# An attention block on one core: a shorter end, V evacuated by pairs, and the softmax offset in rows of its own

## The chip, the cores and the metric

The kernel runs on one core of one Trainium2 chip. The metric is the device time of one execution in microseconds (us). TensorE is called PE, VectorE DVE, ScalarE ACT, GpSimd POOL, and SyncE, whose queue issues most DMAs, SP.

## The reference

```python
B, S, D = x.shape            # 1, 2048, 448, bf16
H = 16; Dh = D // H          # 16 heads of 28
qkv = (x @ wqkv).reshape(B, S, 3, H, Dh).transpose(2, 0, 3, 1, 4)
q, k, v = qkv[0], qkv[1], qkv[2]
scores = jnp.einsum("bhqd,bhkd->bhqk", q, k) * (Dh ** -0.5)
p = softmax(scores, axis=-1)
o = jnp.einsum("bhqk,bhkd->bhqd", p, v)
return o.transpose(0, 2, 1, 3).reshape(B, S, D) @ wo
```

## The kernel before

The 16 heads form four groups `g` of four heads `i`. A head's 28 columns are padded to 32, so that a group fills 128 partitions. The 2048 queries form four blocks `c` of 512 and the keys 16 blocks of 128. A set is one group with one query block; there are 16 sets, and `ORDER` lists them with the last block of the group before the last moved to the second place from the end. Inside a set every head and key block is a unit, a 128 x 512 tile of scores; there are 1024 units.

Scores of a unit are products of `KA` (keys, scaled) with `QP` (queries): `emit_s`, L673. ACT takes two units at a time from a pair of PSUM banks and writes the exponentials `pt` (`do_exp`, L859). DVE takes units one by one from the banks `d0`, `d1` and sometimes `m`, and approximates the exponential by arithmetic on the bits: `do_a` (L874) writes `I`, and for every four units `do_add` (L897) writes two shifted copies `J`. Products with V (`do_pv`, L957) add an ACT unit with the weights `VA`, and a DVE unit three times, with `VA` and its scaled copies `VS`. The four heads of a group write to four column groups, 32 partitions each, of the bank `o`. `VA` holds a column of ones beside each head's 28 columns, so each head's row 28 of `o` is the softmax denominator.

The score has an offset taken off it: K carries four rows of ones (rows 28 to 31 of each head), and the Q side has one row, 28 + c, with a bound on the scores' size below a constant `OFFS`. That bound is computed by `qn_job` (L462): `bound` scales the norms by the largest key norm (`km2`, `z`), halves their bits for a root (`su`), adds `OFFS`, and `place` puts the row into `QP` by DMA (L486). `q_job` (L391) masks Q while it evacuates it (L410) and copies 28 rows of each head into `QP` by DMA (L416). `v_job` (L496) projects two key blocks into one bank, and `evac` copies them into `VA` with two instructions (L517 on DVE, L515 on ACT for three of the pairs).

A finished set is copied out of `o` (L986). A chain of small DMAs gathers its denominators, DVE inverts them, two more DMAs spread the reciprocals over the partitions, and POOL multiplies into `otile(g, c)` (L1008). Products with Wo of the first three query blocks are ordinary jobs (`oproj_job`, L542).

The order of the instructions is not written by hand. A planner in the kernel's own Python code keeps an assumed time for every engine and resource; each job is an `Op` with an assumed duration, needs, a priority and a bank. At each moment the engine that is free first picks what is ready. Whether a unit goes to ACT or DVE is decided in `dve_ok` by who would finish first. Each engine then runs its list in that order, with semaphores where one waits for another. When fewer products than wanted are ready, `dense` puts in a product with a zero operand (L703).

The last set is handled by hand behind the planner's loop (L1146 and on). Two DVE copies bring `o` to SBUF in halves (L1167). `early(tq)` multiplies the other three groups' outputs with Wo for one block of 128 queries (three products, L1163, twelve in all). The halves are transposed in fp32 (L1171), the denominators inverted (L1174) and multiplied (L1175), the result is transposed back in bf16 (L1181) and copied by ACT (L1182). Four products with Wo's last group (L1189) complete the four blocks, DVE and ACT copy them out (L1192, L1194), and two DMAs store them (L1195).

Of the kernel before, what the change touches and what calls it, by code (L numbers as in the profile page):

```python
# [7 lines left out]
ACT = mybir.ActivationFunctionType  # L8
# [29 lines left out]
def kernel(  # L38
# [58 lines left out]
    WO = big.tile([P, G, D], BF16, name="WO")  # L97
    VA = [[big.tile([P, GH, XB, P], BF16, name=f"VA{h}_{b}") for b in range(NXB)] for h in range(2)]
    VS = [[[big.tile([P, GH, XB, P], BF16, name=f"VS{k}_{h}_{b}") for b in range(NXB)] for h in range(2)]
          for k in range(1, NTERM)]  # L100
# [35 lines left out]
    for idx, funcs in enumerate(get_activation_tables(nc.m.arch, ()).values()):  # L136
        if ACT.Exp in funcs and ACT.Identity in funcs:
# [32 lines left out]
    nc.gpsimd.memset(qoff[:], 0.0)  # L170
    for i in range(HG):
        nc.gpsimd.affine_select(out=qoff[:], in_=qoff[:], compare_op=ALU.not_equal, fill=OFFS,
                                base=-(HP * i + Dh), pattern=[[0, 1]], channel_multiplier=1)
    for t in range(3):
        nc.gpsimd.memset(WRAW[t][:, :, D:D + WPAD], 0.0)

    def clear_v(h, b):
        nc.gpsimd.memset(VA[h][b][:], 0.0)
        nc.gpsimd.memset(VA[h][b][:].rearrange("p g t (i e) -> p (g t i) e", e=HP)[:, :, Dh:Dh + 1], 1.0)

# [8 lines left out]

    nc.gpsimd.tensor_copy(out=identf[:], in_=ident[:])  # L190


# [198 lines left out]
    def q_job(g, c, bank, pri, gate=0, split=2):  # L391
# [9 lines left out]
        def evac():  # L401
            if first:
                t = qtt[0] = wk.tile([P, QW], BF16, name="qt0", bufs=1)
            else:
                t = QAt[(g, c)] = big.tile([P, QW], BF16, name=f"QA{c}", tag=f"QA{c}", bufs=1)
            if first:
                nc.vector.tensor_scalar(out=t[:], in0=held[key][:, 0:QW], scalar1=qmask[:, 0:1],
                                        scalar2=qoff[:, 0:1], op0=ALU.mult, op1=ALU.add)
            else:
                nc.vector.tensor_scalar(out=t[:], in0=held[key][:, 0:QW], scalar1=qmask[:, 0:1], scalar2=None,  # L410
                                        op0=ALU.mult)

# [9 lines left out]
        add("DVE", 0.66, evac, need=[key + (split - 1,)], gives=[key], rel=(bank, 2) if first else bank,  # L422
            pri=pri)
# [38 lines left out]
    def qn_job(g, cs, bank, pri, gate=0):  # L462
# [8 lines left out]
        def bound():  # L471
            km2 = wk.tile([P, 1], F32, name="km2")
            nc.vector.tensor_scalar(out=km2[:], in0=kmt[g][:], scalar1=MARG ** 4, scalar2=None, op0=ALU.mult)
# [5 lines left out]
            nc.vector.tensor_scalar(out=su[:], in0=su[:], scalar1=OFFS, scalar2=None, op0=ALU.add)  # L479

# [11 lines left out]
        add("DVE", 1.6, bound, need=[key + (len(cs) - 1,)], gives=[("su",) + key], rel=bank, pri=pri, port=True)  # L492
        add("SP", 1.2 * len(cs), place, need=[("su",) + key] + [("QR", g, c) for c in cs],
            gives=[("QA", g, c) for c in cs], land=1.4, pri=1)

    def v_job(h, kt, bank, pri, gate=0, eng="DVE"):  # L496
# [12 lines left out]
        def evac():  # L509
            ps = held.pop(key)  # L510
            for part in range(2):
                src = ps[:, part * w:(part + 1) * w].rearrange("p (g i e) -> p g i e", g=GH, e=Dh)
                dst = VA[h][b][:].rearrange("p g t (i e) -> p g t i e", e=HP)[:, :, t0 + part, :, 0:Dh]
                if eng == "ACT":
                    nc.scalar.copy(out=dst, in_=src)  # L515
                else:
                    nc.vector.tensor_copy(out=dst, in_=src)  # L517
# [5 lines left out]
        add(eng, 0.62 if eng == "DVE" else 0.5, evac, need=[key + (1,)], gives=[key, ("V", h, kt + 1)], rel=bank, pri=pri)  # L523

    def vs_job(h, b, pri):
        def scale(k):
            nc.vector.tensor_scalar(out=VS[k - 1][h][b][:].rearrange("p g t e -> p (g t e)"),
                                    in0=VA[h][b][:].rearrange("p g t e -> p (g t e)"),
                                    scalar1=WT[k], scalar2=None, op0=ALU.mult)
# [410 lines left out]
    def do_pv(t, ws):  # L940
# [9 lines left out]
        for w in ws:  # L950
            for e in w:
# [4 lines left out]
                SETMM[key] = SETMM.get(key, 0) + 1  # L956
                nc.tensor.matmul(out=o[HP * i:HP * (i + 1), :], lhsT=vt[:, gg, j % XB, HP * i:HP * (i + 1)],  # L957
                                 rhs=e["ap"], start=(SETMM[key] == 1), stop=False, tile_position=(0, HP * i),
# [173 lines left out]

    while cur["oset"] < NSET or any(not late(op) for e in ops for op in ops[e]) or any(k[0] == "O" for k in held):
        e = min(free, key=lambda n: free[n])
# [14 lines left out]
    HW = QW // 2  # L1149
    a = pair_tile(s_bank())  # L1150
    b2 = pair_tile("a%d" % ((cur["u"] + 1) % 2))
    oT = [a[:, 0:QW], b2[:, 0:QW]]
    d0, d1, mb = bank_tile("d0"), bank_tile("d1"), bank_tile("m")
    banks = [d0[:], d1[:], a[:, QW:2 * QW], b2[:, QW:2 * QW]]
    spare = [[VS[k][0][hf][:].rearrange("p g t e -> p (g t e)") for hf in range(2)] for k in range(2)]
    osb_last = [spare[0][hf].bitcast(F32)[:, 0:HW] for hf in range(2)]
    rT = [wk.tile([P, 2, HG], F32, name=f"rT{hf}", bufs=1) for hf in range(2)]
    on = [wk.tile([P, HW], BF16, name=f"on{hf}", bufs=1) for hf in range(2)]
    OTf = [wk.tile([P, HW], BF16, name=f"OTf{hf}", bufs=1) for hf in range(2)]

    def early(tq):
        for gg in range(G - 1):
            nc.tensor.matmul(out=banks[tq][:, 0:D], lhsT=otile(gg, c)[:, tq * P:(tq + 1) * P], rhs=WO[:, gg, :],  # L1163
                             start=(gg == 0), stop=False)

    for hf in range(2):
        nc.vector.tensor_copy(out=osb_last[hf], in_=o[:, hf * HW:(hf + 1) * HW])  # L1167
    early(0)
    for hf in range(2):
        for k in range(2):  # L1170
            nc.tensor.matmul(out=oT[hf][:, k * P:(k + 1) * P], lhsT=osb_last[hf][:, k * P:(k + 1) * P], rhs=identf[:],  # L1171
                             start=True, stop=True)
        ov = oT[hf][:, 0:HW].rearrange("p (t h e) -> p t h e", h=HG, e=HP)
        nc.vector.reciprocal(out=rT[hf][:], in_=ov[:, :, :, Dh])  # L1174
        nc.vector.tensor_tensor(out=on[hf][:].rearrange("p (t h e) -> p t h e", h=HG, e=HP), in0=ov,  # L1175
                                in1=rT[hf][:].unsqueeze(3).to_broadcast([P, 2, HG, HP]), op=ALU.mult)
    early(1)
    tb = [mb[:].bitcast(BF16), bank_tile("o")[:].bitcast(BF16)]
    for hf in range(2):
        for k in range(2):  # L1180
            nc.tensor.transpose(out=tb[hf][:, k * P:(k + 1) * P], in_=on[hf][:, k * P:(k + 1) * P], identity=ident[:])  # L1181
        nc.scalar.copy(out=OTf[hf][:], in_=tb[hf][:, 0:HW])  # L1182
        early(2 + hf)
    rest = sorted({op.gives[0][2] for op in ops["PE"] if late(op)})
    for hf in range(2):
        osb = spare[1][hf][:, 0:2 * D].rearrange("p (t d) -> p t d", t=2)
        for k in range(2):
            tq = 2 * hf + k
            nc.tensor.matmul(out=banks[tq][:, 0:D], lhsT=OTf[hf][:, k * P:(k + 1) * P], rhs=WO[:, G - 1, :],  # L1189
                             start=False, stop=True)  # L1190
            if k == 0:
                nc.vector.tensor_copy(out=osb[:, k, :], in_=banks[tq][:, 0:D])  # L1192
# [44 lines left out]
```

## Time and profile before

| | |
|---|---|
| median of 3 runs | 371.97 us (371.8 to 371.98) |
| the profiled execution | 372.05 us, span 370.2 us |
| granted PE clock | 1.000 |
| busy: PE, DVE, ACT, POOL | 94%, 94%, 95%, 20% |
| instructions: PE, DVE, ACT, POOL | 3487, 648, 391, 93 |
| HBM | 7.58 MB read, 1.96 MB written |

The span goes from the first to the last instruction; the execution's own time is 1.85 us more. A row of a group shows line, engine, operation, what it writes and reads, shapes and count; then busy time in us and the mean of one in ns; then the engine's idle time just before, and what ended it. Busy time counts overlapping instructions of one engine once, so the mean of one can be more than busy time over count. Rows of a timeline and of the chain begin with start and length in us.

### The profile page before, as it was taken

What the parts mean: (1) busy time and instruction counts of PE and PEld (TensorE: products, weight loads), DVE (VectorE), ACT (ScalarE), POOL (GpSimd) and SP (SyncE); (2) the same over time, 40 slices, a digit from 0 to 9 for tenths busy, and PEclk for the clock granted to TensorE, in tenths of its full rate; (3) what the DMA queues carried; (4) which work ended last, traced back from release to release, by engine and by line L of the source; (5) the groups of instructions that cost most, each with busy time, mean ns of one, the idle gap of its engine ahead of it and who ended that gap; (6) DMA issues with size and microseconds to landing.
All of it is one profiled execution on the core that took longest, in us unless ns stands there. A gap on an engine that the chain in (4) does not pass through costs nothing.

```text
span 370.2 us, 8863 instructions
## 1 busy us (share of the span) xinstructions
PE 348.0 (94%) x3487; PEld 112.2 (30%) x3487; DVE 347.5 (94%) x648; ACT 353.0 (95%) x391; POOL 74.4 (20%) x93
## 2 busy tenths in 40 slices
PE   8899998999999999999899999989898999999995
PEld 5443322222333333232222222222222222222222
DVE  7899999999999899999999899999999999999993
ACT  4599999999999999999999999999999999999992
POOL 8931032243010512121010324201010101001010
PEclk9999999999999999999999999999999999999999
DMA  8410011011000001010000001100000001010101
GB/s 256 119 39 12 3 24 35 3 33 36 19 29 32 2 4 38 18 28 30 17 16 3 30 3 54 28 20 14 19 13 4 28 28 56 25 50 21 55 16 50
DMA packets 14994, 12.15 MB, mean 33 GB/s; under 512 B 6780, under 2 KB 13032, under 8 KB 14952
## 3 DMA queue, kind: packets, MB, share of 16 engines
q1 hardware_dynamic: 13400, 10.16, 9.4%
q10 hardware_dynamic: 1040, 1.02, 0.8%
q8 instruction: 27, 0.44, 0.5%
q0 software_dynamic: 512, 0.40, 0.5%
q14 instruction: 15, 0.12, 0.1%
HBM read 7.58 MB, written 1.96 MB: 26 GB/s over the span
## 4 chain that ended last, share of the span: by engine, by line
PE 43%; ACT 38%; DVE 10%; issue 7%; DMA 1%; DVEq 0%; SPq 0%; ACTq 0%
ACT pt L859 38%; PE a L673 16%; PE o L957 12%; PE m L260 5%; DVE I L874 3%; PE m L506 2%; DVE J L897 2%; PE o L590 1%; PE m L542 1%; PE o L703 1%; DVE KA L288 1%; DMA QP<-su 1%; PE d L673 1%; PE m L304 1%; PE a L260 1%
## 5 line engine op out<-in xcount | busy, mean ns | idle before, releaser
L859 ACT ACTIVATE pt<-a 128x1024 bf16<-128x1024 f32 x370 | 340.9, 1137 | 1.3 <-PE a L673 0.7
L874 DVE TENSOR_SCALAR I<-d 128x512 int16<-128x512 f32 x254 | 166.8, 681 | 7.3 <-PE d L673 6.2
L673 PE MATMUL a<-QP,KA 32*128 32x512 bf16 (+1 forms) x730 | 142.5, 381 | 13.3 <-ACT pt L859 12.1
L957 PE MATMUL o<-pt,VA 128*32 128x512 bf16 x740 | 108.3, 386 | 0.5 <-ACT pt L859 0.5
L897 DVE TENSOR_SCALAR J<-I 128x2048 int16<-128x2048 int16 x142 | 100.7, 741 | 0.1
L673 PEld LDWEIGHTS <-KA 32*128 32x128 bf16 (+1 forms) x1024 | 49.2, 91 | 148.5 <-issue 147.8
L673 PE MATMUL d<-QP,KA 32*128 32x512 bf16 x250 | 81.5, 384 | 0.0
L957 PE MATMUL o<-J,VS 128*32 128x512 bf16 x568 | 74.3, 384 | 1.7 <-DVE J L897 1.7
L957 PE MATMUL o<-I,VA 128*32 128x512 bf16 x284 | 66.9, 385 | 0.0
L1008 POOL TENSOR_TENSOR xs<-o_sb,rr 128x512 bf16<-128x512 f32 x12 | 16.6, 1381 | 107.7 <-DMA rr<-scr 92.5
L957 PEld LDWEIGHTS <-VA 128*32 128x32 bf16 x1024 | 24.3, 94 | 40.8 <-issue 40.6
L260 PE MATMUL m<-XT,WRAW 112*32 112x512 bf16 x384 | 29.6, 385 | 0.3 <-DVE QA L410 0.3
L270 POOL TENSOR_TENSOR sq<-QA 128x512 bf16<-128x512 bf16 x15 | 17.5, 1164 | 57.9 <-DVE QA L410 57.9
L270 POOL TENSOR_TENSOR sq<-KA 128x512 bf16<-128x512 bf16 x12 | 16.1, 1340 | 53.6 <-DVE KA L288 53.6
L874 DVE TENSOR_SCALAR I<-m 128x512 int16<-128x512 f32 x30 | 20.5, 682 | 0.9 <-PE m L673 0.6
L957 PEld LDWEIGHTS <-VS 128*32 128x32 bf16 x568 | 16.2, 94 | 15.7 <-issue 15.7
L506 PE MATMUL m<-WRAW,XT 112*128 112x224 bf16 x128 | 17.1, 261 | 0.2
L1008 POOL TENSOR_TENSOR OTL<-o_sb,rr 128x512 bf16<-128x512 f32 x3 | 3.8, 1271 | 60.0 <-DMA rr<-scr 60.0
L703 PE MATMUL o<-zero 128*128 128x512 bf16 x42 | 14.6, 387 | 0.0
L506 PEld LDWEIGHTS <-XT 112*128 112x128 bf16 x128 | 10.2, 97 | 7.1 <-issue 6.2
L673 PE MATMUL m<-QP,KA 32*128 32x512 bf16 x30 | 11.5, 384 | 0.0
L410 DVE TENSOR_SCALAR QA<-m,qmask 128x512 bf16<-128x512 f32 x15 | 11.2, 744 | 0.2 <-PE m L260 0.2
(113 smaller groups left out, 197.3 us busy)
## 6 DMA issues: line engine op xcount, KB each, us to landing
rr<-scr SPq DMA_DIRECT2D x15, 256.0 KB
QP<-QA SPq DMA_DIRECT2D x60, 28.0 KB
out_dram<-osb SPq DMA_DIRECT2D x12, 112.0 KB
WRAW<-in_wqkv_dram SPq DMA_DIRECT2D x3, 392.0 KB
xs<-in_x_dram ACTq DMA_DIRECT2D x4, 224.0 KB
xs<-in_x_dram SPq DMA_DIRECT2D x4, 224.0 KB
QP<-su SPq DMA_DIRECT2D x30, 2.0 KB
out_dram<-VS SPq DMA_DIRECT2D x2, 224.0 KB
```

The lines of the kernel that those rows point to most:

```text
L260: nc.tensor.matmul(out=ps[HP * i:HP * (i + 1), :], lhsT=w[:, cc, h * Dh:h * Dh + HP], rhs=XT[c][cc // 2][:, cc % 2, :], start=(cc == 0), s ...
L270: nc.gpsimd.tensor_tensor(out=t[:], in0=src, in1=src, op=ALU.mult)
L288: nc.vector.tensor_scalar(out=KAt[(g, sc)][:], in0=src, scalar1=kmask[:, 0:1], scalar2=ones[:, 0:1], op0=ALU.mult, op1=ALU.add)
L410: nc.vector.tensor_scalar(out=t[:], in0=held[key][:, 0:QW], scalar1=qmask[:, 0:1], scalar2=None, op0=ALU.mult)
L506: nc.tensor.matmul(out=held[key][:, part * w:(part + 1) * w], lhsT=XT[b][cc // 2][:, cc % 2, t * P:(t + 1) * P], rhs=WRAW[2][:, cc, h * w: ...
L673: nc.tensor.matmul(out=out_ap, lhsT=KAt[(g, j // XB)][r, (j % XB) * P:(j % XB + 1) * P], rhs=q[r, :], start=True, stop=True, tile_position ...
L703: nc.tensor.matmul(out=cur["o"][:], lhsT=zero[:, 0:P], rhs=zero[:], start=False, stop=False, skip_group_check=True)
L859: nc.scalar.activation(out=pt[:], in_=ps[:], func=ACT.Exp, scale=LN2 / 128.0)
L874: nc.vector.tensor_scalar(out=dst, in0=pd[:], scalar1=BIAS, scalar2=0.0, op0=ALU.add, op1=ALU.max)
L897: nc.vector.tensor_scalar(out=r[:, w], in0=ch["I"][:, w], scalar1=float(SHIFT[k]), scalar2=None, op0=ALU.add)
L957: nc.tensor.matmul(out=o[HP * i:HP * (i + 1), :], lhsT=vt[:, gg, j % XB, HP * i:HP * (i + 1)], rhs=e["ap"], start=(SETMM[key] == 1), stop= ...
L1008: nc.gpsimd.tensor_tensor(out=otile(g, c), in0=st["o_sb"][:], in1=st["rr"][:], op=ALU.mult)
```

## The change

The change has four parts.

- V by pairs: `VA` and `VS` have their key block ahead of the group, so that one instruction of 448 columns evacuates a pair.
- Offset rows: `OFFS` gets a row of its own in each `QP` tile, 28 + 3 - c, filled once by sixteen small DMAs on SP's queue. `bound` no longer adds it, and takes both of its factors in one instruction. Q is evacuated without its mask, since only its 28 rows are copied on. The first block of the first group gets the row through `qoff`.
- Planner's figures: the assumed durations of these evacuations and of `bound` follow (0.66 to 0.61, 0.62 to 0.53, 1.6 to 0.94).
- End: the first three groups' products with Wo are jobs (`early_jobs`) that the planner may place among the last units; what is left goes out by `filler`. The last set is not transposed as a whole. Products with a selection matrix `self_` bring the denominators alone across (`work_ps`, four columns each), DVE inverts them, and sixteen fp32 products of a reciprocal's column, repeated 32 times, with the identity spread each over its head's 32 rows. DVE multiplies the untransposed half by that, which gives `OTf` directly. DVE and ACT change places in the last copies.

```diff
-    VA = [[big.tile([P, GH, XB, P], BF16, name=f"VA{h}_{b}") for b in range(NXB)] for h in range(2)]
+    VA = [[big.tile([P, XB, GH, P], BF16, name=f"VA{h}_{b}") for b in range(NXB)] for h in range(2)]
...
+    self_ = const.tile([P, HG], F32, name="self_")
+    offs = const.tile([2, QW], BF16, name="offs")
+    nc.vector.memset(offs[:], OFFS)
...
+    for z in range(2):
+        for c in range(NQC):
+            for k in range(2):
+                nc.sync.dma_start(out=QP[c][k][z][HP * k + Dh + NQC - 1 - c:P:2 * HP, :], in_=offs[:])
...
-                nc.vector.tensor_scalar(out=t[:], in0=held[key][:, 0:QW], scalar1=qmask[:, 0:1], scalar2=None,
-                                        op0=ALU.mult)
+                nc.vector.tensor_copy(out=t[:], in_=held[key][:, 0:QW])
...
-            km2 = wk.tile([P, 1], F32, name="km2")
-            nc.vector.tensor_scalar(out=km2[:], in0=kmt[g][:], scalar1=MARG ** 4, scalar2=None, op0=ALU.mult)
-            nc.vector.tensor_scalar(out=z[:], in0=held.pop(key)[:], scalar1=km2[:, 0:1], scalar2=None, op0=ALU.mult)
+            nc.vector.tensor_scalar(out=z[:], in0=held.pop(key)[:], scalar1=kmt[g][:, 0:1], scalar2=MARG ** 4,
+                                    op0=ALU.mult, op1=ALU.mult)
...
-            nc.vector.tensor_scalar(out=su[:], in0=su[:], scalar1=OFFS, scalar2=None, op0=ALU.add)
...
-            for part in range(2):
-                src = ps[:, part * w:(part + 1) * w].rearrange("p (g i e) -> p g i e", g=GH, e=Dh)
-                dst = VA[h][b][:].rearrange("p g t (i e) -> p g t i e", e=HP)[:, :, t0 + part, :, 0:Dh]
+            src = held.pop(key)[:, 0:2 * w].rearrange("p (r e) -> p r e", e=Dh)
+            dst = VA[h][b][:, t0:t0 + 2, :, :].rearrange("p t g (i e) -> p (t g i) e", e=HP)[:, :, 0:Dh]
...
+    def early_jobs(todo):
+        held.setdefault("early", [None] * XB)
+        c = ORDER[-1][1]
+
+        def mm(tq, bank, gg):
+            if gg == 0:
+                t = pair_tile(bank)[:, QW:2 * QW] if bank[0] == "a" else bank_tile(bank)[:]
+                held["early"][tq] = t
+            nc.tensor.matmul(out=held["early"][tq][:, 0:D], lhsT=otile(gg, c)[:, tq * P:(tq + 1) * P], rhs=WO[:, gg, :],
+                             start=(gg == 0), stop=False)
+
+        for tq, bank in todo:
+            for gg in range(G - 1):
+                add("PE", 0.19 + (D_SWITCH if gg == 0 else 0.0), lambda tq=tq, bank=bank, gg=gg: mm(tq, bank, gg),
+                    pri=2000 + tq, cols=D, need=[("OT", gg, c)] + ([("E", tq, gg - 1)] if gg else []), gives=[("E", tq, gg)],
+                    acq=bank if gg == 0 else None)
...
+        if left() < 12 and chain["cur"] is None and "early" not in held:
+            early_jobs(enumerate(("d0", "d1", "m")))
+        if left() == 0 and ("E", 0) not in held:
+            held[("E", 0)] = True
+            early_jobs([(XB - 1, s_bank())])
...
     for hf in range(2):
         nc.vector.tensor_copy(out=osb_last[hf], in_=o[:, hf * HW:(hf + 1) * HW])
-    early(0)
+    filler(2)
+    work_ps.append(bank_tile("o")[:])
     for hf in range(2):
         for k in range(2):
-            nc.tensor.matmul(out=oT[hf][:, k * P:(k + 1) * P], lhsT=osb_last[hf][:, k * P:(k + 1) * P], rhs=identf[:],
+            nc.tensor.matmul(out=work_ps[hf][:, k * HG:(k + 1) * HG], lhsT=osb_last[hf][:, k * P:(k + 1) * P], rhs=self_[:],
                              start=True, stop=True)
-        ov = oT[hf][:, 0:HW].rearrange("p (t h e) -> p t h e", h=HG, e=HP)
-        nc.vector.reciprocal(out=rT[hf][:], in_=ov[:, :, :, Dh])
-        nc.vector.tensor_tensor(out=on[hf][:].rearrange("p (t h e) -> p t h e", h=HG, e=HP), in0=ov,
-                                in1=rT[hf][:].unsqueeze(3).to_broadcast([P, 2, HG, HP]), op=ALU.mult)
-    early(1)
+        nc.vector.reciprocal(out=rT[hf][:], in_=work_ps[hf][:, 0:2 * HG].rearrange("p (t h) -> p t h", h=HG))
+    filler(2)
     for hf in range(2):
         for k in range(2):
-            nc.tensor.transpose(out=tb[hf][:, k * P:(k + 1) * P], in_=on[hf][:, k * P:(k + 1) * P], identity=ident[:])
-        nc.scalar.copy(out=OTf[hf][:], in_=tb[hf][:, 0:HW])
-        early(2 + hf)
+            for i in range(HG):
+                nc.tensor.matmul(out=work_ps[hf][HP * i:HP * (i + 1), HW + k * P:HW + (k + 1) * P],
+                                 lhsT=rT[hf][:, k, i:i + 1].to_broadcast([P, HP]), rhs=identf[:],
+                                 start=True, stop=True, tile_position=(0, HP * i))
+        nc.vector.tensor_tensor(out=OTf[hf][:], in0=osb_last[hf], in1=work_ps[hf][:, HW:2 * HW], op=ALU.mult)
+    filler(12)
...
-            if k == 0:
+            if k == 1:
                 nc.vector.tensor_copy(out=osb[:, k, :], in_=banks[tq][:, 0:D])
             else:
                 nc.scalar.copy(out=osb[:, k, :], in_=banks[tq][:, 0:D])
```

More of the change, by code (lines that the diff above doesn't have):

```diff
@@ L97 @@
     WO = big.tile([P, G, D], BF16, name="WO")
-    VA = [[big.tile([P, GH, XB, P], BF16, name=f"VA{h}_{b}") for b in range(NXB)] for h in range(2)]
-    VS = [[[big.tile([P, GH, XB, P], BF16, name=f"VS{k}_{h}_{b}") for b in range(NXB)] for h in range(2)]
+    VA = [[big.tile([P, XB, GH, P], BF16, name=f"VA{h}_{b}") for b in range(NXB)] for h in range(2)]
+    VS = [[[big.tile([P, XB, GH, P], BF16, name=f"VS{k}_{h}_{b}") for b in range(NXB)] for h in range(2)]
           for k in range(1, NTERM)]
@@ L172 @@
         nc.gpsimd.affine_select(out=qoff[:], in_=qoff[:], compare_op=ALU.not_equal, fill=OFFS,
-                                base=-(HP * i + Dh), pattern=[[0, 1]], channel_multiplier=1)
+                                base=-(HP * i + Dh + NQC - 1), pattern=[[0, 1]], channel_multiplier=1)
     for t in range(3):
@@ L178, in clear_v @@
         nc.gpsimd.memset(VA[h][b][:], 0.0)
-        nc.gpsimd.memset(VA[h][b][:].rearrange("p g t (i e) -> p (g t i) e", e=HP)[:, :, Dh:Dh + 1], 1.0)
+        nc.gpsimd.memset(VA[h][b][:].rearrange("p t g (i e) -> p (t g i) e", e=HP)[:, :, Dh:Dh + 1], 1.0)
     for h in range(2):
@@ L190 @@
     nc.gpsimd.tensor_copy(out=identf[:], in_=ident[:])
+    nc.gpsimd.memset(self_[:], 0.0)
+    nc.gpsimd.affine_select(out=self_[:], in_=self_[:], compare_op=ALU.not_equal, fill=1.0, base=-Dh,
+                            pattern=[[-HP, HG]], channel_multiplier=1)
     def pair_tile(tg):
@@ L421, in q_job @@
                 acq=bank if p == 0 else None)
-        add("DVE", 0.66, evac, need=[key + (split - 1,)], gives=[key], rel=(bank, 2) if first else bank,
+        add("DVE", 0.66 if first else 0.61, evac, need=[key + (split - 1,)], gives=[key], rel=(bank, 2) if first else bank,
             pri=pri)
@@ L491, in qn_job @@
                 acq=bank if k == 0 else None)
-        add("DVE", 1.6, bound, need=[key + (len(cs) - 1,)], gives=[("su",) + key], rel=bank, pri=pri, port=True)
+        add("DVE", 0.94, bound, need=[key + (len(cs) - 1,)], gives=[("su",) + key], rel=bank, pri=pri, port=True)
         add("SP", 1.2 * len(cs), place, need=[("su",) + key] + [("QR", g, c) for c in cs],
@@ L509, in evac @@
         def evac():
-            ps = held.pop(key)
-            for part in range(2):
-                src = ps[:, part * w:(part + 1) * w].rearrange("p (g i e) -> p g i e", g=GH, e=Dh)
-                dst = VA[h][b][:].rearrange("p g t (i e) -> p g t i e", e=HP)[:, :, t0 + part, :, 0:Dh]
[L514 to L517, printed above, removed]
+            src = held.pop(key)[:, 0:2 * w].rearrange("p (r e) -> p r e", e=Dh)
+            dst = VA[h][b][:, t0:t0 + 2, :, :].rearrange("p t g (i e) -> p (t g i) e", e=HP)[:, :, 0:Dh]
+            if eng == "ACT":
+                nc.scalar.copy(out=dst, in_=src)
+            else:
+                nc.vector.tensor_copy(out=dst, in_=src)
         for p in range(2):
@@ L522, in v_job @@
                 acq=bank if p == 0 else None)
-        add(eng, 0.62 if eng == "DVE" else 0.5, evac, need=[key + (1,)], gives=[key, ("V", h, kt + 1)], rel=bank, pri=pri)
+        add(eng, 0.53 if eng == "DVE" else 0.5, evac, need=[key + (1,)], gives=[key, ("V", h, kt + 1)], rel=bank, pri=pri)
     def vs_job(h, b, pri):
         def scale(k):
-            nc.vector.tensor_scalar(out=VS[k - 1][h][b][:].rearrange("p g t e -> p (g t e)"),
-                                    in0=VA[h][b][:].rearrange("p g t e -> p (g t e)"),
+            nc.vector.tensor_scalar(out=VS[k - 1][h][b][:].rearrange("p t g e -> p (t g e)"),
+                                    in0=VA[h][b][:].rearrange("p t g e -> p (t g e)"),
                                     scalar1=WT[k], scalar2=None, op0=ALU.mult)
@@ L956, in do_pv @@
                 SETMM[key] = SETMM.get(key, 0) + 1
-                nc.tensor.matmul(out=o[HP * i:HP * (i + 1), :], lhsT=vt[:, gg, j % XB, HP * i:HP * (i + 1)],
+                nc.tensor.matmul(out=o[HP * i:HP * (i + 1), :], lhsT=vt[:, j % XB, gg, HP * i:HP * (i + 1)],
                                  rhs=e["ap"], start=(SETMM[key] == 1), stop=False, tile_position=(0, HP * i),
@@ L1131, in late @@
         return op.gives and op.gives[0][0] == "O" and op.gives[0][1] == CL - 1
-    while cur["oset"] < NSET or any(not late(op) for e in ops for op in ops[e]) or any(k[0] == "O" for k in held):
+    def early_jobs(todo):
[12 more added lines that the diff above has]
+                    acq=bank if gg == 0 else None)
+    while cur["oset"] < NSET or ("E", 0) not in held or any(not late(op) and op.gives[0][0] != 'E' for e in ops for op in ops[e]) or any(k[0] == "O" for k in held):
+        if left() < 12 and chain["cur"] is None and "early" not in held:
[3 more added lines that the diff above has]
+            early_jobs([(XB - 1, s_bank())])
         e = min(free, key=lambda n: free[n])
@@ L1149, with filler @@
     HW = QW // 2
[L1150 to L1155, printed above, removed]
+    banks = held["early"]
+    more = [op for op in ops["PE"] if op.gives[0][0] == "E"]
+    def filler(n):
+        for op in more[:n]:
+            op.emit()
+        del more[:n]
@@ L1156 @@
+    spare = [[VS[k][0][hf][:].rearrange("p t g e -> p (t g e)") for hf in range(2)] for k in range(2)]
     osb_last = [spare[0][hf].bitcast(F32)[:, 0:HW] for hf in range(2)]
     rT = [wk.tile([P, 2, HG], F32, name=f"rT{hf}", bufs=1) for hf in range(2)]
-    on = [wk.tile([P, HW], BF16, name=f"on{hf}", bufs=1) for hf in range(2)]
     OTf = [wk.tile([P, HW], BF16, name=f"OTf{hf}", bufs=1) for hf in range(2)]
[L1161 to L1164, printed above, removed]
+    work_ps = [pair_tile("a%d" % ((cur["u"] + 1) % 2))[:, 0:QW]]
```

1 line of the change is left out of this document (removed).

## The prediction

> **What bounds the kernel now.** I read the engine shares first, then the costliest groups, then the chain that ended last, then windows and timelines of the first 40 us and the last 20.
>
> ```profile
> PE 348.0 (94%) x3487; PEld 112.2 (30%) x3487; DVE 347.5 (94%) x648; ACT 353.0 (95%) x391; POOL 74.4 (20%) x93
> L859 ACT ACTIVATE pt<-a 128x1024 bf16<-128x1024 f32 x370 | 340.9, 1137 | 1.3 <-PE a L673 0.7
> L874 DVE TENSOR_SCALAR I<-d 128x512 int16<-128x512 f32 x254 | 166.8, 681 | 7.3 <-PE d L673 6.2
> L874 DVE TENSOR_SCALAR I<-m 128x512 int16<-128x512 f32 x30 | 20.5, 682 | 0.9 <-PE m L673 0.6
> L897 DVE TENSOR_SCALAR J<-I 128x2048 int16<-128x2048 int16 x142 | 100.7, 741 | 0.1
> ```
>
> Three engines stand at 94 to 95%. The softmax is shared out: 370 ACT instructions take two units each (740 of 1024), DVE approximates the other 284. ACT hardly idles between its first exponential and its last, so the kernel has three stretches: until the first exponential, the stream of exponentials, and the tail. Next come the ends of the stream, and its pace where nothing disturbs it (start, length):
>
> ```profile
> 18.87 1.94 ACT L859 ACTIVATE pt<-a 128x1024 bf16<-128x1024 f32 x2
> 143.42 0.73 ACT pt L859
> ...
> 148.84 0.69 ACT pt L859
> ...
> 360.59 1.07 ACT pt L859
> 361.70 0.39 PE o L957 x2
> ```
>
> The two middle rows have six steps between them: 5.42 / 6 = 0.903 us for an exponential. The stream runs from 18.87 to 361.66, 342.8 us; 370 x 0.903 is 334.1. So 8.7 us of it are exponentials that came late, for short products or the few other ACT copies, though the page lists only 1.3 as idle. Behind the last exponential come 8.5 us of tail. The profiled execution took 372.05 us, 1.85 more than its span of 370.2 and 0.08 above the median of 371.97, so a difference in the span is one in the time.
>
> **DVE work removed, and what fills the room.** Groups of instructions, with busy time and mean:
>
> ```profile
> L410 DVE TENSOR_SCALAR QA<-m,qmask 128x512 bf16<-128x512 f32 x15 | 11.2, 744 | 0.2 <-PE m L260 0.2
> L986 DVE COPY o_sb<-o 128x512 f32<-128x512 f32 x15 | 10.2, 683 | 0.4 <-PE o L957 0.4
> L517 DVE CAST VA<-m 128x224 bf16<-128x224 f32 x26 | 8.9, 382 | 0.8 <-PE m L506 0.7
> L547 DVE CAST osb<-m 128x448 bf16<-128x448 f32 x12 | 7.4, 618 | 0.3 <-PE m L542 0.2
> L473 DVE TENSOR_SCALAR km<-kmt 128x1 f32<-128x1 f32 x5 | 0.7, 145 | 0.0
> L479 DVE TENSOR_SCALAR su<-su 128x512 bf16<-128x512 bf16 x5 | 1.5, 295 | 0.2
> ```
>
> Fifteen Q evacuations turn from a masked multiply (11.2/15 = 0.75) into a plain copy (nearest row: 10.2/15 = 0.68): 1.0 us. Thirteen pairs of V evacuations on DVE (8.9/13 = 0.68 a pair) become one instruction of 448 columns (7.4/12 = 0.62): 0.9. Five norm bounds lose two instructions each, 0.7 + 1.5 = 2.2. That is 4.1 us less on DVE.
>
> The planner spends it. In the changed program's instruction order there are 368 exponentials, not 370, and 288 I instructions and 144 J instructions, not 284 and 142. Four I at 187.3/284 = 0.66 and two J at 100.7/142 = 0.71 make 4.1 us: DVE stays as full as it was. ACT loses two exponentials, 2 x 0.903 = 1.8 us. Since the stream sets the length, this is the change's gain: **-1.8**, if ACT stays as well fed. Three V evacuations on ACT, pairs before, become single instructions; each lies between two exponentials and saves under 0.1, which I count at nothing.
>
> A DVE unit needs three products with V (weights 1, 201/256, 159/256) where an ACT unit needs one, so four units moved add 8 column-tiled products.
>
> ```profile
> 22.67 0.55 PE o L957 x8
> ```
>
> That is 0.55 us of PE, hidden where PE waits for ACT; if that cover is gone, 0.55 on the path. The 8.7 us of lateness in the stream will fall differently, because every decision behind the first changed cost shifts; nothing in the trace says which way. I bound it at 1.5 us on both sides, a sixth of it, and take zero.
>
> **The start.** Sixteen small DMAs (two rows of 1 KB) join SP's queue behind the weight loads and ahead of the first Q rows. (The two rows that begin with a window end in clock, DMA share and GB/s.)
>
> ```profile
> 5.58 1.47 SPq L114 DMA_DIRECT2D WRAW<-in_wqkv_dram  x3
> 18.42 2.53 SPq L608 DMA_DIRECT2D QP<-QA  x4
> 38.06 1.10 SPq L486 DMA_DIRECT2D QP<-su  x2
> 12.00:13.00 1.00, 0.89 (x13) 0.34 (x16) 1.00 (x3) 0.29 (x1) 1.00 (x4) 1.00 0.65 168
> 13.00:14.00 1.00, 1.00 (x28) 0.49 (x20) 0.85 (x2) 0.48 (x1) 1.00 (x3) 1.00 0.00 0
> 23.19 0.39 PE L673 MATMUL a<-QP,KA 32*128 32x512 bf16 x2
> ```
>
> The nearest row is L486, the same two-row shape: 0.55 us an issue, 8.8 for sixteen. SP is free from 7.05 to 18.42, 11.4 us. In the instruction order each issue waits for the DMA eight places before it, so the eighth waits for the last weight load, whose data ends in the window 12 to 13 (168 GB/s, then none). From 13.2 nine issues remain: 13.2 + 9 x 0.55 = 18.2, just ahead of 18.42. At the 0.63 of L608's rows it would be 18.9, and the Q rows' four issues would land 0.5 later than now. PE first reads QP at 23.19, 2.2 us behind the end of those issues, about what a landing takes, so of that 0.5 I let 0.4 through as the worst. DVE gets one more short fill, ahead of copies that wait for transposes in any case. POOL gets two small operations and is idle afterwards. Nothing there: **0, at most +0.4**.
>
> **The tail.** The chain from the last exponential on, what DVE does in it, and the DMAs that leave:
>
> ```profile
> 362.09 0.67 PE d L1163 x3
> 362.76 1.00 PE a L1171 x8
> 363.77 0.57 PE d L1163 x3
> 364.34 0.11 PE m L1181 x2
> 364.45 0.57 PE a L1163 x3
> 365.01 0.11 PE o L1181 x2
> 365.13 0.57 PE a L1163 x3
> 365.69 0.20 PE d L1189
> 365.90 0.02 issue
> 365.92 0.62 DVE VS L1192
> 362.13 0.76 DVE L1167 COPY VS<-o 128x256 f32<-128x256 f32 x2 [1.85 <-PE o L957]
> 362.61 1.16 PE L1171 MATMUL a<-identf,VS 128*128 128x128 f32 x8
> 363.36 0.21 DVE L1174 RECIPROCAL rT<-a 128x8 f32<-128x8 f32 x1 [0.47 <-PE a L1171]
> 363.60 0.42 DVE L1175 TENSOR_TENSOR on<-a,rT 128x256 bf16<-128x256 f32 x1
> 366.67 0.81 SPq L1195 DMA_DIRECT2D out_dram<-VS  x2
> ```
>
> PE is busy in every step of it: twelve early products with Wo at 0.57/3 = 0.19 make 2.3 us. Each written fp32 product appears as two records, and eight take 1.00, so a record costs 0.125. The change moves eight early products ahead of the last product with V, and leaves four. In their place comes more fp32 work: four products of four columns, and sixteen that spread a reciprocal over 32 partitions by a 128-column identity. Laid out from 362.61, where the first copied half is seen: four selections (8 records; nearest row L1171, at most 0.125 each, bound by the same 128 weights) end at 363.6. Two early products, 0.38: 364.0. The reciprocals (0.21 each) run beside them. The sixteen spreads follow, and their price is the tail's question. The four spreads of a block stand on different column groups, as the products of L957 do, which took 0.07 each for 512 columns. But the two records of one spread share a group. Bounds: all alike overlap, 0.06 a spread; none do, two records at 0.125, 0.25. I take the middle, one record's time each, 0.125 x 16 = 2.0, since neighbours overlap and the two of one spread don't. Spreads end at 366.0. The multiply (0.42 by L1175, 0.1 ahead of it) ends at 366.5, then two last products and a copy, 0.05 + 0.19 + 0.35 + 0.62 (their starts, one pass through the array, L1192): 367.7, and the second store leaves. Now it leaves at 366.67 + 0.41 = 367.1. So the tail is **+0.6**, between -0.4 (spreads at 0.06: 1.0 less) and +2.6 (2.0 more). What disappears (four bf16 transposes, two ACT copies) was hidden under the twelve early products, and thus buys nothing by itself.
>
> On the spreads the Trainium skill, "TensorE: Matmul & The Clock Gate", Part 3 (The mechanism), says that a weight load overlaps products in flight only where the row group differs. The spreads all use the full row group; by that rule the tail would be at +2.6. The rows of L957 contradict it for bf16, since eight products that share all rows took 0.55; no run so far shows it for fp32.
>
> Of the eight early products inside the stream two stand where five score pairs are still to be issued, one at three, three at one, and two behind the last pair. One of them needs the OT of the set before:
>
> ```profile
> 353.36 1.58 POOL L1008 TENSOR_TENSOR xs<-o_sb,rr 128x512 bf16<-128x512 f32 x1 [17.73 <-DMA rr<-scr]
> ```
>
> It is done at 354.9 now. The order wants it with one score pair left, about three exponentials before the end: 361.66 - 3 x 0.903 = 358.95, so some 4 us of margin if that set ends as long before the end as now (18 exponentials were left at the first product of the last set, and 18 are in the changed order). Sum: -1.8 + 0 + 0.6 = -1.2, from 372.05 to 370.85; against the median, **370.8**.
>
> **Rivals.**
> Serial spreads: no two overlap. The tail is +2.6, and 372.05 - 1.8 + 2.6 = 372.85. For it: the second record of each spread reuses its group, and fp32 weights stand alone in this trace. Against: L957.
> Overlapping spreads: the tail is -0.4, and 369.85. For it: L957's 0.07; against it, the two records.
> PE sets the pace (the slower side): PE has 94%, DVE 94%. Eight products with V (0.55) and eight early ones (1.5) join PE's stream ahead of the last exponential. If PE rather than ACT paces the stream, the two exponentials dropped give nothing back and this 2.05 is on the path: 372.05 + 2.05 + 0.6 = 374.7. It decides from the point where score products start later than the exponential that frees their bank. Against it is the list of waits (total, times, longest), where PE's scores are the ones that wait for ACT:
>
> ```profile
> PE a L673 <- ACT pt L859: 12.1, 36, 0.5
> ```
>
> No gain: the planner's dropped exponentials return as lateness, 1.8 more than 8.7, and only the tail counts: 372.65. For it: DVE is filled back to the brim.
>
> **Numbers.** Forecast 0.45, overlapping spreads 0.17, serial 0.16, PE paces 0.12, no gain 0.10. What this measurement can tell from no change is about 0.2%, 0.74 us. Of the forecast's 0.45, two thirds lie below 371.2 (its own range is 369.3 to 372.3); with the overlapping case and a little of the serial one with luck in the stream, faster gets 0.50. Same: the forecast's other third, half of serial, most of no gain, 0.30. Slower: PE paces, and the rest of serial, 0.20. The range takes the overlapping case with 1 us of luck, 368.8, to the serial one with 0.7 of bad luck, 373.6; PE pacing stays outside.
>
> **What would show it.** Exponentials: 368, with first start near 18.9 and last end near 359.8. Spreads: the time of their group over 16; 0.06, 0.125 or 0.25 decides between the cases. SP's last offset issue before 18.5, and PE not waiting for QP. The forecast is wrong if the stream is not about 1.8 us shorter (then look for exponentials more than 0.95 apart, and what PE did there), or if the tail from the last exponential is not 8.1 to 11.1 us.

## The result, and the profile after

The changed kernel takes 369.95 us (median of five runs, 369.44 to 370.24), against 371.97 before: 2.0 us less, ratio 0.9942 with a 95% interval of 0.9928 to 0.9957. The forecast was 370.8. The profiled execution took 370.24 us, its span is 368.4; before, it was 372.05 and 370.2. Below, "after" is the changed kernel.

The page of after, engine shares and the costliest groups:

```profile
PE 349.5 (95%) x3522; PEld 111.6 (30%) x3522; DVE 347.3 (94%) x632; ACT 350.4 (95%) x384; POOL 72.7 (20%) x95
L864 ACT ACTIVATE pt<-a 128x1024 bf16<-128x1024 f32 x368 | 339.2, 1125 | 1.1 <-PE a L678 0.4
L879 DVE TENSOR_SCALAR I<-d 128x512 int16<-128x512 f32 x260 | 170.1, 682 | 5.3 <-PE d L678 3.9
L902 DVE TENSOR_SCALAR J<-I 128x2048 int16<-128x2048 int16 x144 | 102.5, 744 | 0.2
L879 DVE TENSOR_SCALAR I<-m 128x512 int16<-128x512 f32 x28 | 19.0, 679 | 0.1
```

ACT has 2.6 us less, DVE is as busy as before, and PE has 1.5 us more. The groups view has the two evacuations that got shorter: Q (11.2 us before) and V on DVE (8.9).

```profile
L420 DVE CAST QA<-m 128x512 bf16<-128x512 f32 x15 | 10.2, 682 | 0.0
L522 DVE CAST VA<-m 128x448 bf16<-128x448 f32 x13 | 8.0, 618 | 0.2
```

The ends of the stream of exponentials, from ACT's timelines:

```profile
19.08 1.94 ACT L864 ACTIVATE pt<-a 128x1024 bf16<-128x1024 f32 x2
358.79 1.02 ACT L864 ACTIVATE pt<-a 128x1024 bf16<-128x1024 f32 x1
```

| profiled execution, us | before | after | difference |
|---|---|---|---|
| until the first exponential | 18.87 | 19.08 | +0.21 |
| stream | 342.78 | 340.73 | -2.05 |
| of it, number x 0.903 | 334.11 | 332.30 | -1.81 |
| of it, lateness | 8.67 | 8.43 | -0.24 |
| tail behind the last exponential | 8.58 | 8.60 | 0.0 |

"Lateness" is, as in the prediction, the stream's length less its exponentials at 0.903 us each. So the gain lies in the stream, and nearly all of it is two exponentials. The tail did not move.

The tail of after, from the chain of waits and the timelines of PE, DVE and SP:

```profile
359.67 0.30 PE d L1146
359.96 0.19 PE m L1146
360.15 0.32 PE o L962 x2
360.48 0.29 PE d L1146
360.77 0.19 PE a L1146
361.00 0.61 PE a L1196 x4
361.61 0.45 PE o L1196 x4
362.05 0.40 PE a L1146 x2
362.38 0.64 PE L1203 MATMUL a<-identf,rT 128*32 128x128 f32 x16
362.84 0.62 PE L1203 MATMUL o<-identf,rT 128*32 128x128 f32 x16
363.09 0.42 DVE L1206 TENSOR_TENSOR OTf<-VS,a 128x256 bf16<-128x256 f32 x1 [0.80 <-PE a L1203]
363.53 0.42 DVE L1206 TENSOR_TENSOR OTf<-VS,o 128x256 bf16<-128x256 f32 x1
364.85 0.86 SPq L1219 DMA_DIRECT2D out_dram<-VS  x2
```

From product to product PE has few gaps, as before, but its work is now selections (L1196), spreads (L1203) and four early products (L1146) instead of transposes and twelve early products.

The 0.21 us ahead of the first exponential are there before PE reaches anything of the change. The chains of before and of after begin with the same zero products and transposes, and the transposes already begin 0.15 us later:

```profile
1.19 4.30 PE o L590 x10
5.49 0.89 PE d L568 x16
```

```profile
1.19 4.45 PE o L595 x10
5.64 0.96 PE d L573 x16
```

### The profile page after: what moved, and what is told of

It reads as the page before. It is cut to its first block, busy times and chain, and to the rows that moved or that the text cites. A ratio compares the mean times of both kernels' runs of the same rounds, so it can differ in the third digit from the quotient of the medians.

```text
span 368.4 us, 8926 instructions
## 1 busy us (share of the span) xinstructions
PE 349.5 (95%) x3522; PEld 111.6 (30%) x3522; DVE 347.3 (94%) x632; ACT 350.4 (95%) x384; POOL 72.7 (20%) x95
## 4 chain that ended last, share of the span: by engine, by line
PE 52%; ACT 30%; DVE 10%; issue 6%; DVEq 0%; ACTq 0%
ACT pt L864 30%; PE a L678 19%; PE o L962 16%; PE m L270 7%; DVE I L879 4%; DVE J L902 4%; PE m L547 1%; PE m L513 1%; PE o L595 1%; PE o L708 1%; PE d L678 1%; PE m L314 1%; DVE osb L552 1%; PE d L573 1%; PE a L270 1%
## 5 line engine op out<-in xcount | busy, mean ns | idle before, releaser
L879 DVE TENSOR_SCALAR I<-d 128x512 int16<-128x512 f32 x260 | 170.1, 682 | 5.3 <-PE d L678 3.9
L678 PE MATMUL a<-QP,KA 32*128 32x512 bf16 (+1 forms) x726 | 141.6, 381 | 11.2 <-ACT pt L864 10.1
L962 PE MATMUL o<-pt,VA 128*32 128x512 bf16 x736 | 105.5, 385 | 0.0
L902 DVE TENSOR_SCALAR J<-I 128x2048 int16<-128x2048 int16 x144 | 102.5, 744 | 0.2
L678 PE MATMUL d<-QP,KA 32*128 32x512 bf16 x256 | 84.0, 384 | 0.4 <-DVE I L879 0.3
L962 PE MATMUL o<-J,VS 128*32 128x512 bf16 x576 | 78.7, 385 | 0.4 <-DVE J L902 0.4
L280 POOL TENSOR_TENSOR sq<-KA 128x512 bf16<-128x512 bf16 x12 | 13.2, 1102 | 59.2 <-DVE KA L298 59.2
L962 PEld LDWEIGHTS <-VS 128*32 128x32 bf16 x576 | 18.1, 94 | 19.7 <-issue 19.7
L513 PEld LDWEIGHTS <-XT 112*128 112x128 bf16 x128 | 10.2, 97 | 7.1 <-issue 7.1
L991 DVE COPY o_sb<-o 128x512 f32<-128x512 f32 x15 | 10.3, 684 | 1.4 <-PE o L962 1.3
L547 PE MATMUL m<-WO,xs 128*128 128x448 bf16 x36 | 10.9, 358 | 0.3 <-DVE I L879 0.2
```

Source lines behind the costliest of these rows:

```text
L280: nc.gpsimd.tensor_tensor(out=t[:], in0=src, in1=src, op=ALU.mult)
L513: nc.tensor.matmul(out=held[key][:, part * w:(part + 1) * w], lhsT=XT[b][cc // 2][:, cc % 2, t * P:(t + 1) * P], rhs=WRAW[2][:, cc, h * w: ...
L547: nc.tensor.matmul(out=held[key][:, 0:D], lhsT=otile(g, c)[:, tq * P:(tq + 1) * P], rhs=WO[:, g, :], start=(g == 0), stop=(g == G - 1))
L678: nc.tensor.matmul(out=out_ap, lhsT=KAt[(g, j // XB)][r, (j % XB) * P:(j % XB + 1) * P], rhs=q[r, :], start=True, stop=True, tile_position ...
L879: nc.vector.tensor_scalar(out=dst, in0=pd[:], scalar1=BIAS, scalar2=0.0, op0=ALU.add, op1=ALU.max)
L902: nc.vector.tensor_scalar(out=r[:, w], in0=ch["I"][:, w], scalar1=float(SHIFT[k]), scalar2=None, op0=ALU.add)
```

## The experiments

Twelve kernels were run, each compared with before on the same chip, where the median of before lay between 371.89 and 372.31 us. The table gives the median, the ratio to before, and of the one profiled execution the exponentials, the lateness (with 0.903; the expectations count with 0.9035, which makes it 0.2 less) and the tail. One execution need not lie at the median of its kernel: that of e3 was 0.6 us faster than the median and that of e5 0.9 faster, that of e7 1.7 slower. So differences in lateness of less than about 1 us between two rows show little.

| run | us | ratio (95%) | exponentials | lateness | tail |
|---|---|---|---|---|---|
| before | 371.97 | | 370 | 8.7 | 8.58 |
| after | 369.95 | 0.9942 (0.9928-0.9957) | 368 | 8.4 | 8.60 |
| e1 end alone | 372.26 | 1.0007 (0.9996-1.0017) | 370 | 8.7 | 8.52 |
| e2 old end | 369.93 | 0.9942 (0.9928-0.9956) | 368 | 8.0 | 8.59 |
| e3 figures alone | 370.75 | 0.9963 (0.9950-0.9977) | 368 | 8.9 | 8.60 |
| e4 old figures | 371.85 | 0.9996 (0.9985-1.0007) | 370 | 8.1 | 8.52 |
| e5 after, factor 0.98 | 370.23 | 0.9943 (0.9929-0.9957) | 364 | 11.1 | 8.76 |
| e6 after, factor 0.94 | 378.04 | 1.0152 (1.0125-1.0180) | 360 | 24.1 | 8.39 |
| e7 before, factor 0.98 | 370.16 | 0.9934 (0.9916-0.9952) | 366 | 11.8 | 8.60 |
| e8 spreads in pairs | 369.73 | one run | 368 | 7.7 | 8.67 |
| e9 after, factor 1.01 | 370.81 | 0.9972 (0.9950-0.9995) | 366 | 11.4 | 7.98 |
| e10 Q and offset rows alone | 370.47 | 0.9959 (0.9945-0.9974) | 368 | 8.5 | 8.61 |
| e11 V alone | 371.14 | 0.9979 (0.9968-0.9990) | 370 | 7.3 | 8.59 |
| e12 another order | 370.71 | 0.9969 (0.9957-0.9981) | 368 | 8.0 | 9.16 |

### e1 and e2: the end

```diff
 # e1: before, with after's self_, early_jobs, filler and the code behind the loop
 # e2: after, with before's code behind the loop, no self_, no early_jobs
```

> Before, with the new end alone (early products as jobs, selections, reciprocals spread by products); V, the Q side and the planner's figures stay as before. Theory A (the split of the units makes the gain, the two ends take the same time): still 370 exponentials, the stream as before, and a tail of 8.5 to 8.7 us behind the last exponential, so 371.7 to 372.3 us. Rival B (the gain is the end: eight early products of 0.19 us leave the tail): the tail is 1 to 1.5 us shorter than the 8.58 of before, so 370.4 to 371.0 us.

> After, with the old end (transposes, twelve early products behind the last product with V); the rest of the change stays. Theory A: 368 exponentials, the stream of after, 369.7 to 370.3 us. Rival B: the tail is 1 to 1.5 us longer than that of after, 370.9 to 371.5 us.

The end alone gives nothing that can be measured (1.0007), and with the old end in its place the whole gain remains (0.9942). All four tails lie between 8.5 and 8.6 us. Rival B falls.

### e3 and e4: the planner's figures

```diff
 # e3: before, three assumed durations; e4: after, the same three back
-        add("DVE", 0.66, evac, ...
+        add("DVE", 0.66 if first else 0.61, evac, ...
-        add("DVE", 1.6, bound, ...
+        add("DVE", 0.94, bound, ...
-        add(eng, 0.62 if eng == "DVE" else 0.5, evac, ...
+        add(eng, 0.53 if eng == "DVE" else 0.5, evac, ...
```

> Before, with the planner's three new figures alone (0.61, 0.53, 0.94): no instruction gets shorter, but the split becomes 368 exponentials, 288 I and 144 J. Theory A (the dropped exponentials are paid by the DVE work that the change removes): DVE has 4.1 us more to do than before, falls behind, and score banks come free late; the lateness of the stream rises from 8.4 us to 10 to 12, and the time is 371.5 to 374 us. Rival C (DVE had room all along, the figures alone make the gain): lateness 8 to 9 us, 369.9 to 370.5 us.

> After, with the planner's old figures: all instructions are as short as in after, but the split is 370 exponentials, 284 I, 142 J as before. Theory A: the freed 4.1 us stay idle on DVE and ACT paces the stream; 370 exponentials of 0.904 us, lateness 7.5 to 8.5 us, 371.2 to 372.2 us. Rival D (the shorter evacuations shorten the stream by themselves, since exponentials were late on account of DVE): lateness 6 to 7 us, 369.8 to 370.7 us.

The page of e3:

```profile
L859 ACT ACTIVATE pt<-a 128x1024 bf16<-128x1024 f32 x368 | 339.5, 1127 | 1.1 <-PE d L673 0.3
L874 DVE TENSOR_SCALAR I<-d 128x512 int16<-128x512 f32 x260 | 169.4, 680 | 4.1 <-PE d L673 3.1
L897 DVE TENSOR_SCALAR J<-I 128x2048 int16<-128x2048 int16 x144 | 101.9, 739 | 0.2
```

With no instruction shortened, the split of after comes out, DVE does the added I and J on top of all its old work, and the kernel is 0.37% faster. The lateness is 8.9 in the profiled execution and by estimate 9.4 at the median, below the 10 to 12 of theory A. DVE had room: in the stream of before, the time in which no DVE instruction runs adds up to 13.0 us (the stream less the union of DVE's instructions), in e3 to 10.1. Most of that room lay in the middle of the stream: between 110 and 350 us DVE idles 8.3 us in before and 3.6 in e3. Theory A falls in its reason, that the freed DVE time pays for the split; rival C is nearer, though 370.75 is above its 370.5. In e4 all instructions are short and DVE idles 16.4 us, and the time is that of before. So the shorter instructions by themselves, at the old split, bring nothing in that order of the work. Rival D falls for this order (e11 below is faster at the old split).

### e5, e6, e7, e9: more on DVE

```diff
-SLOW_V = 1.03
+SLOW_V = 0.98        # e5 in after, e7 in before; e6: 0.94, e9: 1.01 in after
```

> After, with one constant changed: the factor on every assumed DVE duration, 1.03, becomes 0.98. The split becomes 364 exponentials, 296 I and 148 J. Theory E (the split sets the time as long as DVE has idle time left; after has 11.7 us of it in the stream, and 8 I at 0.66 and 4 J at 0.71 take 8.1 of that): four exponentials of 0.904 us less than after, lateness 8 to 9 us, 366.1 to 367.3 us. Theory A (DVE is as full as can be at 368): DVE's results come late, lateness 11 to 14 us, 369.3 to 373 us.

> After, with the factor 0.94: 360 exponentials, 304 I, 152 J. 16 I and 8 J more than after take 16.2 us, more than the 11.7 us that DVE idles in the stream. Theory E: DVE paces the stream now, lateness 12 to 18 us over 325.3, 367 to 372 us, so no better than with 364. Without a limit from DVE or PE it would be 362.7 us.

> Before, with the factor 0.98 alone: 366 exponentials, 292 I, 146 J; no instruction changes. Theory E: 13.0 us of DVE's idle time in the stream take the 8.1 us added; four exponentials less than before, 368.0 to 369.3 us, below after with nothing of the change but another split. Theory A (the split needs the shorter evacuations): lateness 11 us or more, 371 us or more.

> After, with the factor on the assumed DVE durations at 1.01 instead of 1.03: 366 exponentials, 292 I, 146 J, between after (368) and the run with 364, which took the same time. If lateness grows evenly with the split (8.2 at 368, 10.9 at 364, so 9.5 here), 366 x 0.9035 + 9.5 + first start and tail as in after: 369.4 to 370.0 us, no gain that can be told from after. If lateness stays at 8.2 until DVE's room is used up, 368.1 to 368.7 us and the fastest of all.

Pushed on by one constant, the split buys no more: at 366 and 364 the lateness is 11.1 to 11.8 us (at the medians, by estimate, about 10 in e7 and 12 in e5 and e9), which takes back what the exponentials give, and at 360 it is 24.1. The page and the list of waits of e6:

```profile
L864 ACT ACTIVATE pt<-a 128x1024 bf16<-128x1024 f32 x360 | 336.8, 1051 | 11.9 <-PE a L678 5.8
ACT pt L864 <- PE a L678: 5.8, 13, 1.1
ACT pt L864 <- PE d L678: 4.2, 11, 0.9
```

ACT now waits for scores, 10 us in these two rows against 0.7 in after (0.4 and 0.3). Theory E was right on the direction of e6 and wrong on the size (378.0 for 367 to 372), and wrong for e5, e7 and e9, where it left lateness at 8 to 9 us as long as DVE idles; e5's 370.23 lies in the range of theory A, e7's 370.16 between the two, and e9's 370.81 above both of its forecasts. In e5 DVE still idles 8.2 us in the stream, in e6 9.8.

What sets those waits in e6 can be read from its trace: in the main it is DVE. The chain of waits by engine, from the pages of after, e5 and e6 in this order, and who holds up PE in e6:

```profile
PE 52%; ACT 30%; DVE 10%; issue 6%; DVEq 0%; ACTq 0%
PE 41%; DVE 34%; ACT 17%; issue 6%; DMA 1%; DVEq 0%; ACTq 0%
DVE 65%; PE 19%; ACT 8%; issue 6%; DMA 1%; SPq 0%; POOL 0%; DVEq 0%; ACTq 0%
PE d L678 <- DVE I L879: 3.5, 6, 1.0
PE o L962 <- DVE o_sb L991: 2.4, 8, 0.8
PE o L962 <- DVE J L902: 1.7, 3, 0.9
```

PE waits 7.6 us for DVE in these three rows, against 0.7 in after. The 9.8 us that DVE idles in e6 hide this, because 8 of them lie before 110 us or behind 350: between the two DVE is busy 238.25 of 240 us, while PE idles 12.5. In the same 240 us DVE idles 8.3 in before, 4.5 in after and 3.4 to 4.3 in e5, e7 and e9. So the room in the middle was half gone at 368 exponentials, and pushing on found little more there. This fits the lateness, but which single waits make that of e5, e7 and e9 was not separated.

e7 is the sharpest comparison: before, with one constant changed and nothing else, has a ratio of 0.9934 (0.9916 to 0.9952), the same as after within the intervals. Its runs scatter more, 368.9 to 371.9 us. None of the four beats after beyond its interval.

### e8: the order of the spreads

```diff
-        for k in range(2):
-            for i in range(HG):
+        for i in range(HG):
+            for k in range(2):
```

> After, with the two loops around the spreading products swapped, so that two products for the same column group follow each other instead of four for different groups. If column groups overlap in fp32 and one group's products don't, the sixteen spreads take 1.3 to 1.9 us of PE instead of 0.9, and the tail grows by 0.3 to 0.9 us. If the order makes no difference (weights are what bounds them), 0.9 us and the same tail.

The chain of e8:

```profile
361.92 0.67 PE a L1203 x16
```

Eight spreads take 0.67 us in the chain where they took 0.62 in after, and the tail of this single run is 8.67. With pairs in one column group the spreads cost nearly the same, so a change of column group from each product to the next is not what makes them cheap. What does was not tested further.

### e10 and e11: the other parts alone

```diff
 # e10: before, with offs, its sixteen DMAs, the shorter bound, tensor_copy for Q, figures 0.61 and 0.94
 # e11: before, with VA and VS by key block, one evacuation for a pair, figure 0.53
```

> Before, with the offset rows, the shorter bound and the unmasked Q copy (3.2 us less DVE work) and their figures; V and the end as before. The split becomes 368, 288, 144. Split theory: 369.9 to 370.7 us, nearly the whole gain. Sixteen more DMAs on SP at the start: no later first exponential than 18.6 to 19.4 us.

> Before, with V in pairs and its figure alone (0.9 us less DVE work, three shorter ACT copies). The split stays at 370, 284, 142. Split theory: 371.6 to 372.3 us, no gain. If work removed from DVE counted by itself, 0.9 of 4.1 us of the gain of 2.0: 371.5 us.

e10 flips the split and takes 370.47, as foreseen, with the first exponential at 18.88 as in before. Its sixteen DMAs on SP's timeline:

```profile
7.25 10.72 SPq L175 DMA_DIRECT2D QP<-offs  x16
18.43 2.47 SPq L611 DMA_DIRECT2D QP<-QA  x4
```

They end at 17.97, and the Q rows leave at 18.43 where they left at 18.42. e11 keeps the split of before and is still 0.21% faster, with a lateness of 7.3. The split theory does not hold for it; a share of the gain for DVE work removed (371.5) doesn't give it in full either. Its twelve runs lie between 370.6 and 371.9 us, and the profiled one, 370.8, is below their median. Since e4 has this same shorter work, and more, without a gain, I take it for the luck of one order, but that is an argument and not shown.

### e12: the same split in another order

```diff
-D_EXP = 0.912
+D_EXP = 0.913
```

> After, with the assumed duration of an exponential at 0.913 instead of 0.912 us: the split stays at 368, 288, 144, and all decisions behind the first close call may fall differently. It shows by how much another order of the same work moves the time: lateness 7.5 to 9 us as in the other runs with 368, so 369.3 to 370.8 us; if the order by itself matters more than the split, anything from 368 to 372.

The work and the split are those of after, and it takes 370.71. Its tail is 9.16 us, 0.56 longer. The chain of e12:

```profile
363.19 0.49 PE m L1146 x2
363.68 0.57 PE a L1146 x3
364.25 0.39 PE d L1213 x2
```

Five early products were left over here, and the last `filler` put them ahead of the last four products, while DVE's multiplied half had long been there (363.24 by its timeline). So the new end has a price that depends on the order. By the starts of L1146 the planner placed three of the twelve early products among the last units here, for a tail of 9.16 us; it placed five in e5 (8.76), eight in after (8.60) and ten in e9 (7.98). Between them the order is not strict: e1, e4 and e6 placed seven, and their tails are 8.39 to 8.52.

## Why the prediction was right or wrong

**The stream: right, for half the reason.** It was to lose 1.8 us and lost 2.05: 1.8 for the two exponentials, 0.2 of lateness, well inside the 1.5 allowed. The three DVE terms came out as worked out: Q 11.2 to 10.2, V 8.9 to 8.0, and two instructions gone from each bound. Wrong was the sentence that the planner spends the freed 4.1 us: e3 has the same split and 1.3 of the 2.0 us of gain without them, because DVE idled 13 us. The change acts in the main through what the planner believes of DVE. That a share of 94% leaves no room was read into the page; the trace of before has the room, 8.3 us of it between 110 and 350 us.

**The start: right.** SP issues the sixteen DMAs from 7.37 to 18.47 (the sum said 18.2 to 18.9), the Q rows leave at 18.63, right behind the result that they carry, and PE waits for none of them. Of the 0.21 us in after, 0.15 are there when the first transposes begin. The first exponential begins at 18.88 to 19.42 in the runs with the sixteen DMAs and at 18.62 to 19.22 in those without, so it moves from run to run by more than these 0.21 us.

**The tail: mis-sized, +0.6 forecast, 0.0 measured.** The term that failed is the price of a spread. I took 0.125 us, since the two records of one spread would not overlap; the timeline of after has the second half's spreads begin 0.46 us behind the first's, 0.058 for each of eight, which was the cheap end of the range. That is the rival with overlapping spreads, which had the tail at -0.4 and the time at 369.85; the measured 369.95 is closer to it than to the forecast of 370.8. For the profiled execution the sum gave 370.85 and 370.24 was measured: the tail has 0.6 too much in it and the stream 0.25, the start 0.2 too little. What lies between -0.4 and 0.0: the last product with V starts 0.27 us behind the last exponential instead of 0.05, because two early products (359.67 and 359.96 in the chain above) stand ahead of it, and the last copies give the rest. On the rule of the Trainium skill ("TensorE: Matmul & The Clock Gate", Part 3, The mechanism), by which loads overlap products only in other row groups and the tail would be at +2.6, the measurement decides against it: 32 records, all on the full row group, went by in 1.1 us (362.38 to 363.46), where one after another at 0.125 they would take 4.0.

**What the end was worth.** That the end as a whole brings nothing is shown by e1 and e2: the two ends take the same 8.5 to 8.6 us. That the removed transposes and copies by themselves bring nothing fits this, but was not tested alone. Eight early products, 1.5 us, left the tail, and it is no shorter, because the selections, spreads and waits between PE and DVE took their place: from the last product with V to the multiplied halves it is still one chain.

**PE sets the pace** did not happen: PE's scores still wait for ACT (10.1 us in after, 12.1 before). e6 shows a neighbouring case, with 8 exponentials fewer than after: ACT waits for scores because PE waits for DVE.

**No gain** did not happen at 368 exponentials, where the lateness is 8.4; two and four exponentials further on (e9, e5) the dropped exponentials do return as lateness in the main, as that rival had it.

**What stays open.** After is 0.2% below e3, e10 and e12, about as much as the intervals are wide. e12 shows that another order of the same work can cost 0.8 us by the medians; between the two profiled executions it is 0.5, with a tail 0.56 longer. The 0.8 us by which e3 is slower than after could be such an order too. Whether the shorter instructions add anything of their own beyond the split, these runs can't tell.

## What to carry to other kernels

In a kernel whose order comes from a planner, an edit changes the work and what the planner believes of it; run the new assumed durations alone, with the old instructions, before putting the gain down to the instructions. A busy share of 94% on three engines doesn't tell how much room the second one has: add up its idle time stretch by stretch, since the total can hide that the middle is full (e6), and price by experiment how far it can be filled. Work moved out of a tail is a gain only as far as what takes its place is cheaper: two quite different ends came out within 0.1 us here.

## What the runs showed of the hardware

An fp32 product of 128 weights costs the same with 4 moving columns as with 128: each is two records, and by the start times of the traces a record follows the one before it by 0.11 us in L1196 of after (4 columns) and, but for the first step, in L1171 of before (128 columns). A stationary operand of 32 columns was far cheaper: 16 records with 128 moving columns went by in 0.46 us, 0.03 each, with little regard to which column groups followed each other (0.67 against 0.62 us in the chain). In after and in e8 alike, these records start in bundles of four, and a bundle follows the one before it by 0.11 us in most steps, as one record of 128 columns does. So four records of 32 stationary columns cost what one of 128 costs; other widths were not run.
